# The last layer of a three-layer kernel as seven block products, with its operands loaded earlier and one item's transposes moved

## The chip, the core and the metric

The kernel runs on one core of one Trainium2 chip. TensorE does the matmuls and writes PSUM, which has eight banks here, b0 to b7, of 512 float32 columns on 128 partitions. VectorE (DVE) and ScalarE (ACT) work on SBUF and PSUM. SyncE (SP) issues every DMA. The metric is the device time of one execution in microseconds, given as the median of several runs. The trace is of one execution that was profiled.

## What is computed

```python
def _moe2_ref(x, w_in, w_out):
    h = x @ w_in
    g = h * (1.0 / (1.0 + np.exp(-h)))
    return (g @ w_out).astype(np.float32)
def reference(**kwargs):
    ...
    attn_out = _attn_ref(**attn_kwargs)
    ...
    x = np.ascontiguousarray(attn_out.transpose(0, 2, 1, 3)).reshape(B * S, H * D)
    x = _moe_ref(x=x, **moe_kwargs)
    return _moe2_ref(x=x, **moe2_kwargs)
```

Attention over 64 positions at a time comes first (4 sequences of 576 tokens, 8 heads of 64), then two pairs of layers: `_moe_ref` (512 to 2048 features, a leaky rectifier, back to 512) and `_moe2_ref`, shown above. There are 2304 tokens. The weights arrive as float64. "The last layer" below is `g @ w_out` of `_moe2_ref`, with 2304 x 2048 by 2048 x 512. "The third layer" is `x @ w_in` of the same function.

## The kernel before

Tokens are cut into 6 tiles of 384 (`TN`), the 2048 features into 16 blocks of 128. Every value of a matmul is split into two float32r parts, high and low: ScalarE casts the high part and VectorE subtracts it from the value (`parts`, L271 to L273). A product is then three matmuls: high by high, high by low, low by high.

Attention is 24 items, four for each tile. An item's scores (`mm_s`, L179), softmax (`softmax`, `rescale`), transposes (`mm_t`, L224, in two halves of three), the copies of these (`keep_t`) and the product with the values (`mm_v`, L240) are written out by hand: the first in the string `START`, the others inside the loop over the steps `f` of the first layer (`mlp_h1`, L334; `mlp_g1`; `join_g1`, L352). Item 8 (`EARLY`) is the first that stands in the loop: its transposes come at f = 0 of tile 1. Each engine works through its own instructions in the order in which the program issues them.

The third layer is already done by seven block products instead of eight: two tiles make a pair (`u`), `unit(u, c, ...)` computes four output blocks of 128 x 384 by `product` (L453, six matmuls of 128 x 384 each), and the eight units of a pair take their right sides from combinations of weights. Its results pass the Silu in `finish` (L468) and go to DRAM (L470). A hook between any two products runs what a table `plan` has for that slot: `slot(u, c, h)` counts seven slots for each unit. The weights of the last layer are converted beforehand (`aside`), kept in DRAM, and fetched and split during the third pair (`back`).

The last layer takes a tile at a time, with 16 blocks:

```python
        for n, (a, b) in enumerate(((gh, oh), (gh, ol), (gl, oh))):
            for i in banks:
                nc.tensor.matmul(acc2[t][i], a[:, i * P:(i + 1) * P], b,
```

`a` is the stationary operand, 128 columns of the Silu's output, and `b` the moving one, 128 x 512 of the weights. So a step is nine matmuls (L530), and `split_g2(n + 3)` runs three steps ahead. One product of the third layer, `last_product`, is done after the first step. At the end `put` copies the sums out (L539) and stores them.

Of the kernel before, what the change touches and what calls it, by code (L numbers as in the profile page):

```python
# [20 lines left out]
q0 w1 s0a q1 q2 s0b w2 s1a v0 s1b c1 q3 s2a v1 z s2b t0 h1 q4 s3a p0 v2 w3 s3b t1 c2 p1 v3 q5 s4a w4 s4b  # L21
t2 h2 v4 p2 s5a w5 s5b t3 v5 p3 c3 w6 s6a t4 s6b M0 p4 h3 G0 c4 s7a t5 s7b M1 p5 w7 G1 h4 t6
s8a M2 p6 s8b c5 G2 t7 M3 p7 h5 G3
# [8 lines left out]
def attention_two_mlps(ctx, tc, q, k, v, w_in1, w_out1, alpha, w_in2, w_out2, out):  # L32
# [186 lines left out]
    def mm_t(n):  # L219
        it = items[n]  # L220
        for hf in range(2):
# [4 lines left out]
    def keep_t(n):  # L226
        it = items[n]
        for hf in range(2):
# [243 lines left out]
    def last_product(prev):  # L472
        product(prev["u"], prev["c"], B22, prev["a"])
        finish(prev["u"], prev["c"], 0, 1, prev["a"], room(turn_c(), name="c"))
# [33 lines left out]
    gl2, gs2, acc2 = {}, {}, {}  # L508
    turn_2h, turn_2l = Turn(range(0, 4)), Turn(range(4, 8))

    def load_g2(n):
        if n >= NTILE * KF or n in gl2:
            return
        g = gl2[n] = stg.tile([P, TN], F32, name="gf", tag="st")
        nc.sync.dma_start(out=g, in_=gd2[divmod(n, KF)])

    def split_g2(n):
        if n >= NTILE * KF:
            return
        g = gl2.pop(n)  # L520
        gh, gl = room(turn_2h(), None, F32R, "gh"), room(turn_2l(), None, F32R, "gl")
        parts(g, gh, gl)
        gs2[n] = (gh, gl)

    def sums(t, f, banks):
        oh, ol = wt["o2", f]
        gh, gl = gs2[t * KF + f]
        for n, (a, b) in enumerate(((gh, oh), (gh, ol), (gl, oh))):
            for i in banks:
                nc.tensor.matmul(acc2[t][i], a[:, i * P:(i + 1) * P], b,  # L530
                                 start=(f == 0 and n == 0), stop=(f == KF - 1 and n == 2))

    def put(t, i, parts):
        r0 = t * TN + i * P
        w = DM // parts
        for j in range(parts):
            c = slice(j * w, (j + 1) * w)
            osb = cv.tile([P, w], F32, name="osb", tag="cv")
            (nc.scalar.copy if (i + j) % 2 else nc.vector.tensor_copy)(osb, acc2[t][i][:, c])  # L539
            nc.sync.dma_start(out=out[r0:r0 + P, c], in_=osb)  # L540

    def mlp_o2(t, f):
# [256 lines left out]
```

## Time and profile before

| | |
|---|---|
| median of 3 runs | 876.23 us (875.97 to 878.31) |
| the profiled execution | 877.78 us, of which the span of the trace is 876.0 us |
| TensorE busy | 846.5 us (97% of the span), 5472 matmuls and as many weight loads |
| VectorE, ScalarE busy | 489.0 us (56%), 414.0 us (47%) |

The span runs from the first to the last instruction of the trace. "PE" is TensorE's matmul, "PEld" its weight load, and "SPq" SyncE's queue of DMA issues. A busy time of an instruction reaches from its start to its end, so instructions that overlap count twice in a mean but not in a busy time.

### The profile page before, as it was taken

How to read it: one execution, taken by the hardware profiler on the slowest of the kernel's cores; microseconds unless marked ns; L12 is line 12 of the kernel's file. 1: busy time of each engine (PE TensorE's matmuls, PEld its weight loads, DVE VectorE, ACT ScalarE, POOL GpSimd, SP SyncE). 2: the span in 40 equal slices, each digit the busy share in tenths (PEclk: the TensorE clock that was granted, in tenths of full speed). 3: DMA queues.
4: the chain of work that ended last, by engine and by line, in shares of the span. 5: the costliest groups of instructions: out<-in, count | busy, mean ns of one | idle time of the engine just before them, and what ended most of it. 6: DMA issues, size and time to landing. Idle time of an engine off the chain costs nothing.

```text
span 876.0 us, 15271 instructions
## 1 busy us (share of the span) xinstructions
PE 846.5 (97%) x5472; PEld 794.2 (91%) x5472; DVE 489.0 (56%) x1193; ACT 414.0 (47%) x1080; POOL 3.1 (0%) x20
## 2 busy tenths in 40 slices
PE   5689999999999999999999999999999999999998
PEld 4569999999999999999999999999999888888886
DVE  5677875467676776567665474644644233233232
ACT  5576666667665532244323355645765322222221
POOL 1000000000000000000000000000000000000000
PEclk9899999999999999999999999999999999999999
DMA  8457743477655557765575345455565443344341
GB/s 263 155 154 248 217 141 127 131 244 218 216 176 190 160 182 251 266 193 192 195 255 158 111 156 180 157 204 192 192 193 179 124 134 120 112 131 124 110 129 61
DMA packets 103467, 152.01 MB, mean 174 GB/s; under 512 B 10336, under 2 KB 87392, under 8 KB 103392
## 3 DMA queue, kind: packets, MB, share of 16 engines
q1 hardware_dynamic: 103392, 151.04, 53.9%
q8 instruction: 43, 0.70, 0.3%
q14 instruction: 32, 0.26, 0.1%
HBM read 99.62 MB, written 51.38 MB: 172 GB/s over the span
## 4 chain that ended last, share of the span: by engine, by line
PE 91%; DVE 3%; ACT 3%; issue 2%; DMA 1%; SPq 0%; ACTq 0%; DVEq 0%
PE acc L395 23%; PE acc L530 22%; PE h L334 21%; PE qa L453 11%; PE qd L453 5%; PE pa L240 3%; PE qb L453 3%; PE pa L224 2%; PE pa L179 2%; ACT pr L198 1%; DMA kT<-in_k_dram 0%; DVE pr L193 0%; DVE cva L265 0%; ACT a L341 0%; ACT g L342 0%
## 5 line engine op out<-in xcount | busy, mean ns | idle before, releaser
L334 PE MATMUL h<-x,i 128*128 128x384 f32 x1152 | 207.4, 337 | 1.4 <-ACT g L342 1.4
L273 DVE TENSOR_TENSOR gl<-gf,gh 128x384 fp32r<-128x384 f32 x192 | 106.3, 556 | 171.2 <-PE acc L530 122.4
L334 PEld LDWEIGHTS h<-x,i 128*128 128x128 f32 x1152 | 199.0, 188 | 3.1 <-ACT g L342 2.7
L272 ACT CAST gh<-gf 128x384 fp32r<-128x384 f32 x192 | 97.7, 515 | 212.4 <-PE acc L530 124.8
L395 PE MATMUL acc<-gh,o 128*128 128x384 f32 x768 | 148.6, 334 | 0.0
L530 PE MATMUL acc<-o,gh 128*128 128x512 f32 x576 | 147.2, 389 | 0.0
L395 PEld LDWEIGHTS acc<-gh,o 128*128 128x128 f32 x768 | 134.5, 188 | 0.2 <-ACT gh L272 0.2
L530 PEld LDWEIGHTS acc<-o,gh 128*128 128x128 f32 x576 | 108.1, 188 | 22.3
L453 PE MATMUL qa<-v,w2i 128*128 128x384 f32 x576 | 108.2, 334 | 1.0 <-ACT fk L458 1.0
L453 PEld LDWEIGHTS qa<-v,w2i 128*128 128x128 f32 x576 | 100.5, 188 | 1.7 <-ACT fk L458 1.7
L395 PE MATMUL acc<-gl,o 128*128 128x384 f32 x384 | 82.0, 334 | 0.0
L530 PE MATMUL acc<-o,gl 128*128 128x512 f32 x288 | 81.8, 389 | 0.0
L341 ACT ACTIVATE a<-h 128x384 f32<-128x384 f32 x96 | 47.0, 490 | 69.1 <-PE h L334 49.3
L352 DVE SCALAR_TENSOR_TENSOR g<-a,nalpha,g 128x384 f32<-128x384 f32 x96 | 58.5, 614 | 33.2 <-ACT g L342 33.2
L395 PEld LDWEIGHTS acc<-gl,o 128*128 128x128 f32 x384 | 67.9, 188 | 0.0
L198 ACT ACTIVATE pr<-pr,nm 128x128 f32<-128x128 f32 x144 | 56.2, 395 | 24.5 <-DVE nm L193 24.5
L530 PEld LDWEIGHTS acc<-o,gl 128*128 128x128 f32 x288 | 54.1, 188 | 11.2
L453 PE MATMUL qd<-v,w2i 128*128 128x384 f32 x288 | 57.6, 334 | 0.0
L453 PEld LDWEIGHTS qd<-v,w2i 128*128 128x128 f32 x288 | 50.6, 188 | 0.0
L342 ACT ACTIVATE g<-h 128x384 f32<-128x384 f32 x96 | 46.6, 485 | 0.0
L265 DVE SCALAR_TENSOR_TENSOR cva<-s,cva 128x512 uint32<-128x512 uint32 x64 | 44.4, 693 | 2.2
L267 DVE SCALAR_TENSOR_TENSOR cva<-s,cva 128x512 uint32<-128x512 uint32 x64 | 44.3, 692 | 2.2
(64 smaller groups left out, 729.7 us busy)
## 6 DMA issues: line engine op xcount, KB each, us to landing
gf<-g SPq DMA_DIRECT2D x192, 192.0 KB, 2.4
g<-g SPq DMA_DIRECT2D x96, 192.0 KB, 3.9
g<-c SPq DMA_DIRECT2D x96, 192.0 KB, 1.9
s<-in_moe_w_in_dram SPq DMA_DIRECT2D x32, 512.0 KB, 5.2
s<-in_moe_w_out_dram SPq DMA_DIRECT2D x32, 512.0 KB, 4.8
ve<-in_v_dram SPq DMA_DIRECT2D x24, 192.0 KB, 3.7
x<-x SPq DMA_DIRECT2D x24, 192.0 KB, 2.0
xq<-x SPq DMA_DIRECT2D x12, 384.0 KB, 4.6
```

The source lines that it names most:

```text
L198: nc.scalar.activation(out=pr[:, j, :], in_=pr[:, j, :], func=AF.Exp, bias=nm[:, j:j + 1], scale=-1.0, accum_out=it["sm"][:, hf * HB + j:h ...
L265: nc.vector.scalar_tensor_tensor(out=a, in0=s[:, :, 1], scalar=0xC0000000, in1=a, op0=ALU.bitwise_and, op1=ALU.bitwise_or)
L267: nc.vector.scalar_tensor_tensor(out=a, in0=s[:, :, 0], scalar=29, in1=a, op0=ALU.logical_shift_right, op1=ALU.bitwise_or)
L272: nc.scalar.copy(hi, src)
L273: nc.vector.tensor_tensor(out=lo, in0=src, in1=hi.bitcast(F32), op=ALU.subtract)
L334: nc.tensor.matmul(h, w[:, kk, :], x, start=(kk == 0 and n == 0), stop=(kk == KD - 1 and n == 2))
L341: nc.scalar.activation(out=a, in_=h, func=AF.Relu, scale=-1.0)
L342: nc.scalar.activation(out=g, in_=h, func=AF.Relu)
L352: nc.vector.scalar_tensor_tensor(out=g, in0=a, scalar=nalpha[:, f:f + 1], in1=g, op0=ALU.mult, op1=ALU.add)
L395: nc.tensor.matmul(acc1[t][i], a[:, i * P:(i + 1) * P], b, start=(f == 0 and n == 0), stop=(f == KF - 1 and n == 2))
L453: nc.tensor.matmul(o, w[:, a, k0], b, start=start and kk == 0 and n == 0, stop=kk == 1 and n == 2, skip_group_check=True)
L530: nc.tensor.matmul(acc2[t][i], a[:, i * P:(i + 1) * P], b, start=(f == 0 and n == 0), stop=(f == KF - 1 and n == 2))
```

## The change

It has three parts.

The last layer is done by seven block products for each pair of tiles. The output of a pair is four blocks of 384 x 256. The left sides are blocks of the Silu's output (A11, A12, A22) and sums of them (S1 to S4), the right sides are blocks of the weights (B11, B21, B22) and combinations (T1 to T4) of 128 x 256. A product has 8 steps of nine matmuls of 128 x 256, so a pair has 56 steps and the layer 168. The order of the products is A11, S3, S2, A12, S1, A22, S4. Three of them start on empty banks, and four add to banks of an earlier one after a copy of it was taken (`fork2`). The right sides are combined in the earlier layers (`variants`) and kept in DRAM; 37 of the 56 are fetched and split in the third pair of the third layer and 19 (`late`) in the last layer.

The blocks A11 and A21 of the first pair are loaded in the third layer's last two units, from `slot(2, 6, 1)` on, and A22 and A12 in the last layer. `last_product` now comes after two steps.

The transposes are issued half by half. For items 0 to 7 the order of instructions stays the same on every engine. Item 8's move from f = 0 to f = 2.

```diff
-q0 w1 s0a q1 q2 s0b w2 s1a v0 s1b c1 q3 s2a v1 z s2b t0 h1 q4 s3a p0 v2 w3 s3b t1 c2 p1 v3 q5 s4a w4 s4b
+q0 w1 s0a q1 q2 s0b w2 s1a v0 s1b c1 q3 s2a v1 z s2b t0a t0b h1 q4 s3a p0 v2 w3 s3b t1a t1b c2 p1 v3 q5 s4a w4 s4b
...
+    STEPS = 7 * KH
+    SEQ = (A11, S3, S2, A12, S1, A22, S4)
+    gb, gs2, acc2, side2 = {}, {}, {}, {}
...
+    def load_g2(u, x, c):
...
+        gb[u, x, c] = g
+        nc.sync.dma_start(out=g, in_=gd2[2 * u + i, c + KH * jj])
...
+    def sum_g2(u, x, c):
...
+        a, b, op, o = {S3: (A11, A21, ALU.subtract, None), S1: (A21, A22, ALU.add, A21),
+                       S2: (S1, A11, ALU.subtract, A11), S4: (A12, S2, ALU.subtract, S2)}[x]
...
+        nc.vector.tensor_tensor(out=o, in0=gb[u, a, c], in1=gb[u, b, c], op=op)
+        gb[u, x, c] = o
...
+        if n < 4:
+            t = tp.tile([P, 2, TN], F32R, name="gs", tag="ts") if n == 0 else stg.tile([P, 2, TN], F32R, name="gs", tag="st")
+            gh, gl = t[:, 0, :], t[:, 1, :]
+        else:
+            r = turn_gs()
+            gh, gl = room(r, None, F32R, "gh"), room(r + 1, None, F32R, "gl")
+        parts(gb[u, x, c], gh, gl)
         gs2[n] = (gh, gl)
...
+    def sums(n, chunks):
...
+        gh, gl = gs2[n]
+        w = wt["o2", c, v]
+        for a, b in ((gh, 0), (gh, 1), (gl, 0)):
+            for i in chunks:
+                nc.tensor.matmul(acc2[u, v][i], a[:, i * P:(i + 1) * P], w[:, b, :],
...
+    def banks2(u, v):
+        at = {A11: (2, 3) if u % 2 else (4, 6), A12: (7, 1), S3: (5, 0)}[v]
+        x, y = bank(at[0], "acc"), bank(at[1], "acc")
+        side2[u, v] = (x, y[:, :HD])
+        acc2[u, v] = (x[:, :HD], x[:, HD:], y[:, :HD])
...
+    def fork2(u, v):
...
+        for o, c in zip(side2[u, v], (slice(0, 2 * HD), slice(2 * HD, 3 * HD))):
+            nc.scalar.copy(s[:, c], o)
+        return s
...
+    def put(u, i, j, v, s=None, part=(0, 1)):
...
+            if s is not None:
+                nc.vector.tensor_tensor(out=x, in0=o, in1=x, op=ALU.add)
+            elif k == 0:
+                nc.scalar.copy(x, o)
+            else:
+                nc.vector.tensor_copy(x, o)
...
+        if n >= NU * STEPS - 3:
+            if n < NU * STEPS - 1:
...
             for i in range(NC):
+                for nn in range(n - 2, n + 1):
+                    sums(nn, (i,))
+                if i:
+                    put(u, 0, 1, v, None, (i - 1,))
...
+        if v == A11:
+            forks["p1"] = fork2(u, v)
...
+        elif v == A12:
+            put(u, 0, 0, v, forks["p1"])
+        elif v == S3:
+            forks["p7"] = fork2(u, v)
+        elif v == S2:
+            forks["u2"] = fork2(u, v)
+        elif v == S1:
+            put(u, 1, 1, v, forks["p7"])
+        elif v == A22:
+            put(u, 1, 0, v, forks["u2"])
+        else:
+            put(u, 0, 1, v)
...
+    def around2(n):
+        u, m = divmod(n, STEPS)
+        for x, first in ((A11, 36), (A21, 32), (A22, 40), (A12, 48)):
+            if 0 <= m - first < KH:
+                load_g2(u + 1, x, m - first)
+        if u == 0 and 4 <= n < 4 + KH:
+            load_g2(0, A12, n - 4)
+        for x, first in ((S3, -4), (S1, 2), (S2, 7), (S4, 34)):
+            for uu in (u, u + 1):
+                c = n - (uu * STEPS + first)
+                if uu == 0 and x == S3:
+                    continue
+                if uu == 0 and x in (S1, S2):
+                    c -= 2 if x == S1 else 3
+                if 0 <= c < KH:
+                    sum_g2(uu, x, c)
...
         elif x == "t":
-            mm_t(n)
-            keep_t(n)
+            hf = (int(w[-1] == "b"),)
+            rescale(n, hf)
+            mm_t(n, hf)
+            keep_t(n, hf)
...
+        def combine():
...
+            combos(x[:, :HD], x[:, HD:], y[:, :HD], y[:, HD:], t)
+            d = dram.tile([P, 7, HD], F32, name=f"w2o_{c}")
+            nc.sync.dma_start(out=d[:, 0, :], in_=x[:, :HD])
+            nc.sync.dma_start(out=d[:, 1:3, :], in_=y.rearrange("p (k d) -> p k d", d=HD))
+            nc.sync.dma_start(out=d[:, 3:, :], in_=t)
...
         def fetch():
+            a = held["o2", m] = cv.tile([P, HD], F32, name="cva", tag="cv")
+            nc.sync.dma_start(out=a, in_=parked[c, v])
...
+        def split():
+            s = wroom((56 + m) % 64, [P, 2, HD], F32R, "w2o")
+            parts(held.pop(("o2", m)), s[:, 0, :], s[:, 1, :])
+            wt["o2", c, v] = s
+        return fetch, split
...
+    late = list(range(4 * KH, 4 * KH + 3)) + list(range(5 * KH, 7 * KH))
+    for i, m in enumerate(m for m in range(7 * KH) if m not in late):
+        plan.setdefault(slot(2, 0, 3) + i * 9 // 8, []).append(rights[m][0])
+        plan.setdefault(slot(2, 1, 0) + i * 9 // 8, []).append(rights[m][1])
...
-                    rescale(n, (1,) if n == EARLY else (0, 1))
-                    mm_t(n)
+                    if n > EARLY:
+                        rescale(n)
+                        mm_t(n)
                     if f:
                         keep_v(n - 1)
-                    keep_t(n)
+                    if n > EARLY:
+                        keep_t(n)
...
+                    if n == EARLY:
+                        for hf in ((0,), (1,)):
+                            rescale(n, hf)
+                            mm_t(n, hf)
+                            keep_t(n, hf)
                     rescale(n + 1)
...
-        plan.setdefault(slot(2, 6, 3 + i), []).append(lambda i=i: load_g2(i))
+    at = lambda g, f: plan.setdefault(g, []).append(f)
+    for i, c in enumerate(range(KH)):
+        at(slot(2, 6, 1) + i * 3 // 4, lambda c=c: load_g2(0, A11, c))
+        at(slot(2, 6, 6) + i * 3 // 4, lambda i=i: load_g2(0, A21, i))
     for i in range(3):
-        plan.setdefault(slot(2, 7, 3 + i), []).append(lambda i=i: (split_g2(i), load_g2(i + 4)))
+        if i < 2:
+            at(slot(2, 7, 4) + i, lambda i=i: split_g2(i))
+        at(slot(2, 7, 2) + i, lambda i=i: sum_g2(0, S3, i))
 
...
-    for n in range(NTILE * KF):
+    finish(prev["u"], prev["c"], 1, 1, c22)
+    split_g2(2)
+    for n in range(NU * STEPS):
+        if n == 2:
+            last_product(prev, stg.tile([P, TN], F32, name="c", tag="st"))
+            for c in range(KH):
+                load_g2(0, A22, c)
         split_g2(n + 3)
-        load_g2(n + 7)
-        mlp_o2(*divmod(n, KF))
-        if n == 0:
-            last_product(prev)
-            finish(prev["u"], prev["c"], 1, 1, c22)
+        around2(n)
+        if n < 5:
+            sum_g2(0, S3, 3 + n)
+        for i, m in enumerate(late):
+            if n == 14 + i * 30 // len(late):
+                rights[m][1]()
...
+        step2(n)
+        for i, m in enumerate(late):
+            if n == 12 + i * 30 // len(late):
+                rights[m][0]()
```

On TensorE the order at the ninth item (number 8; `pa<-ident,pr` are its transposes, `h<-x,i` the first layer's matmuls) was, before:

```order
L240 MATMUL pa<-pt,ve 64x64 x2
L179 MATMUL pa<-kT,qT 64x128 x12
L224 MATMUL pa<-ident,pr 128x128 x6
L334 MATMUL h<-x,i_277 128x384 x2
L334 MATMUL h<-x,i_278 128x384
L334 MATMUL h<-x,i_277 128x384 x2
```

and the same transposes now stand here:

```order
L335 MATMUL h<-x,i_450 128x384
L335 MATMUL h<-x,i_449 128x384 x2
L335 MATMUL h<-x,i_450 128x384
L224 MATMUL pa<-ident,pr 128x128 x6
L335 MATMUL h<-x,i_647 128x384 x2
L335 MATMUL h<-x,i_648 128x384
```

The transposes have moved behind the h products of two steps, 24 matmuls, of which the last ones are shown, and stand ahead of the third.

On TensorE the end of the third layer (`qa<-v,w2i`) and the start of the last (`acc<-o` before, `acc<-w2o` now; `gs` holds both parts of one of the first four left sides) was:

```order
L453 MATMUL qa<-v,w2i 128x384 x12
L530 MATMUL acc<-o_7730,gh 128x512 x3
L530 MATMUL acc<-o_7731,gh 128x512 x3
L530 MATMUL acc<-o_7730,gl 128x512 x3
L453 MATMUL qa<-v,w2i 128x384 x6
L530 MATMUL acc<-o_7766,gh 128x512 x3
```

and is now:

```order
L454 MATMUL qa<-v,w2i 128x384 x12
L564 MATMUL acc<-w2o,gs 128x256 x18
L454 MATMUL qa<-v,w2i 128x384 x6
L564 MATMUL acc<-w2o,gs 128x256 x18
L564 MATMUL acc<-w2o,gh 128x256 x6
L564 MATMUL acc<-w2o,gl 128x256 x3
```

One step of nine matmuls of 512 columns ahead of the last third-layer product has become two steps of nine matmuls of 256.

On VectorE the first tiles of the last layer (`gl` is the low part of a left side, `osb` a result that is copied out) were:

```order
L463 TENSOR_TENSOR c<-qa,fk 128x384
L273 TENSOR_TENSOR gl<-gf,gh 128x384 x16
L539 COPY osb<-acc 128x512 x2
L273 TENSOR_TENSOR gl<-gf,gh 128x384 x16
L539 COPY osb<-acc 128x512 x2
```

and at the start of the second pair VectorE now has (the rows with `g<-g` and `s<-g` are the sums S1, S2 and S3):

```order
L539 TENSOR_TENSOR s_9611<-g 128x384
L539 TENSOR_TENSOR g<-g 128x384
L274 TENSOR_TENSOR gl<-g,gh 128x384
L539 TENSOR_TENSOR s_9627<-g 128x384
L539 TENSOR_TENSOR g<-g 128x384
L274 TENSOR_TENSOR gl<-g,gh 128x384
L539 TENSOR_TENSOR g<-g 128x384
L274 TENSOR_TENSOR gl<-s_9507,gh 128x384
L539 TENSOR_TENSOR g<-g 128x384
L274 TENSOR_TENSOR gl<-s_9524,gh 128x384
L539 TENSOR_TENSOR g<-g 128x384
L274 TENSOR_TENSOR gl<-s_9541,gh 128x384
```

Up to two sums have come between one split and the next.

## Rows read from the trace of the kernel before

**Rows 1.** The page: the head, and the chain that ended last by line.
```profile
span 876.0 us, 15271 instructions
...
PE acc L395 23%; PE acc L530 22%; PE h L334 21%; PE qa L453 11%; PE qd L453 5%; PE pa L240 3%; PE qb L453 3%; PE pa L224 2%; PE pa L179 2%; ACT pr L198 1%; DMA kT<-in_k_dram 0%; DVE pr L193 0%; DVE cva L265 0%; ACT a L341 0%; ACT g L342 0%
```

**Rows 2.** Busy time by stage; start and end, length, engines with instructions, granted clock.
```profile
300.00:486.00 186.00, 186.00 (x1074) 185.77 (x1073) 123.09 (x249) 66.84 (x153) 0.00 (x0) 1.00 0.66 213
486.00:680.00 194.00, 192.98 (x1107) 191.65 (x1106) 99.45 (x192) 107.82 (x243) 0.00 (x0) 1.00 0.52 175
675.19:872.34 197.15, 197.15 (x871) 163.04 (x870) 59.81 (x106) 52.19 (x103) 0.00 (x0) 1.00 0.39 119
```

**Rows 3.** Timeline, TensorE, last layer: start, length, what, how many.
```profile
675.19 1.55 PE L530 MATMUL acc<-o,gh 128*128 128x512 f32 x6
680.42 1.52 PE L530 MATMUL acc<-o,gh 128*128 128x512 f32 x6
682.46 1.52 PE L530 MATMUL acc<-o,gh 128*128 128x512 f32 x6
```

**Rows 4.** Timeline, TensorE, third layer.
```profile
663.75 1.20 PE L453 MATMUL qa<-v,w2i 128*128 128x384 f32 x6
664.79 1.20 PE L453 MATMUL qd<-v,w2i 128*128 128x384 f32 x6
```

**Rows 5.** Slices of 10 ns: weight loads under way (x) in the first layer.
```profile
106.14:106.15 0.01, 0.01 (x1) 1.00 0.99 410
106.24:106.25 0.01, 0.01 (x2) 1.00 1.40 563
106.41:106.42 0.01, 0.01 (x1) 1.00 0.93 308
106.42:106.43 0.01, 0.01 (x2) 1.00 1.27 461
```

**Rows 6.** VectorE and ScalarE by form: busy time, mean ns of one.
```profile
L273 DVE TENSOR_TENSOR gl<-gf,gh 128x384 fp32r<-128x384 f32 x192 | 106.3, 556 | 171.2 <-PE acc L530 122.4 <-ACT gh L272 40.9 <-PE acc L395 7.6
L463 DVE TENSOR_TENSOR c<-qd,fk 128x384 f32<-128x384 f32 x24 | 13.3, 554 | 11.7 <-PE qd L453 8.5 <-ACT c L468 3.2
L273 DVE TENSOR_TENSOR w2i<-ts,w2i 128x256 fp32r<-128x256 f32 x32 | 13.4, 419 | 7.5 <-ACT w2i L272 7.5
L539 DVE COPY osb<-acc 128x512 f32<-128x512 f32 x11 | 7.1, 687 | 9.7 <-PE acc L530 9.7
L341 ACT ACTIVATE a<-h 128x384 f32<-128x384 f32 x96 | 47.0, 490 | 69.1 <-PE h L334 49.3 <-issue 16.0 <-ACT gh L272 1.7
```

**Rows 7.** Timeline, VectorE: two operations back to back.
```profile
674.08 0.55 DVE L463 TENSOR_TENSOR c<-qd,fk 128x384 f32<-128x384 f32 x1
674.55 0.55 DVE L273 TENSOR_TENSOR gl<-gf,gh 128x384 fp32r<-128x384 f32 x1
```

**Rows 8.** Timeline, TensorE and VectorE, around the ninth item's transposes.
```profile
63.76 0.55 PE L224 MATMUL pa<-ident,pr 128*128 128x128 f32 x3
66.34 0.52 PE L224 MATMUL pa<-ident,pr 128*128 128x128 f32 x3 [2.03 <-DVE pr L216]
...
64.69 0.61 DVE L352 SCALAR_TENSOR_TENSOR g<-a,nalpha,g 128x384 f32<-128x384 f32 x1
65.63 0.56 DVE L216 TENSOR_TENSOR pr<-pr,rs 128x384 f32<-128x384 f32 x1
```

**Rows 9.** Timeline, the end of the program.
```profile
871.95 0.39 PE L530 MATMUL acc<-o,gl 128*128 128x512 f32 x1
872.38 0.43 DVE L539 COPY osb<-acc 128x256 f32<-128x256 f32 x1 [2.03 <-PE acc L530]
872.84 0.37 ACT L539 COPY osb<-acc 128x256 f32<-128x256 f32 x1 [1.91 <-DVE osb L539]
```

**Rows 10.** The page: DMA issues; size, median us from issue to landing.
```profile
gf<-g SPq DMA_DIRECT2D x192, 192.0 KB, 2.4
s<-in_moe_w_out_dram SPq DMA_DIRECT2D x32, 512.0 KB, 4.8
```

More of the change, by code (lines that the diff above doesn't have):

```diff
@@ L217, in rescale, with mm_t @@
                                     op=ALU.mult)
-    def mm_t(n):
+    def mm_t(n, halves=(0, 1)):
         it = items[n]
-        for hf in range(2):
+        for hf in halves:
             pb = it[f"b{hf}"] = att_bank()
@@ L224, in mm_t, with keep_t @@
                 nc.tensor.transpose(pb[:, j * P:(j + 1) * P], it[f"p{hf}"][:, j, :], ident)
-    def keep_t(n):
+    def keep_t(n, halves=(0, 1)):
         it = items[n]
-        for hf in range(2):
+        for hf in halves:
             pt = it[f"pt{hf}"] = room(turn_pt(), [P, HB, P], F32, "pt")
@@ L517, in split_g2 @@
     def split_g2(n):
-        if n >= NTILE * KF:
+        if n >= NU * STEPS:
             return
-        g = gl2.pop(n)
-        gh, gl = room(turn_2h(), None, F32R, "gh"), room(turn_2l(), None, F32R, "gl")
-        parts(g, gh, gl)
-        gs2[n] = (gh, gl)
[L525 to L542, printed above, removed]
-        if f == 0:
-            acc2[t] = [bank(i, "acc") for i in ((1, 5, 0) if t % 2 else (4, 6, 7))]
-        if t == NTILE - 1 and f >= KF - 3:
-            if f == KF - 1:
-                for i, ff in ((0, 2), (0, 1), (1, 2), (1, 1), (0, 0), (1, 0), (2, 2), (2, 1), (2, 0)):
-                    sums(t, f - ff, [i])
-                    if ff == 0:
-                        put(t, i, 2 if i == NC - 1 else 1)
-            return
-        sums(t, f, range(NC))
-        if f == KF - 1:
-            for i in range(NC):
-                put(t, i, 1)
+        u, m = divmod(n, STEPS)
@@ new lines, in attention_two_mlps, with step2 @@
+    ready = []
+    forks = {}
+    def step2(n):
+        u, m = divmod(n, STEPS)
+        k, c = divmod(m, KH)
+        v = SEQ[k]
+        if c == 0:
+            if v in (A11, A12, S3):
+                banks2(u, v)
+            elif v == A22:
+                acc2[u, v], side2[u, v] = acc2[u, S3], side2[u, S3]
+            else:
+                acc2[u, v], side2[u, v] = acc2[u, A11], side2[u, A11]
+        if n >= NU * STEPS - 3:
+            if n < NU * STEPS - 1:
+                return
+            for i in range(NC):
+                for nn in range(n - 2, n + 1):
+                    sums(nn, (i,))
+                if i:
+                    put(u, 0, 1, v, None, (i - 1,))
+            return
+        sums(n, range(NC))
+        if c < KH - 1:
+            return
+        if v == A11:
[8 more added lines that the diff above has]
+            put(u, 1, 1, v, forks["p7"])
+        elif v == A22:
+            put(u, 1, 0, v, forks["u2"])
+        else:
+            put(u, 0, 1, v)
@@ new lines, in around2 @@
+    def around2(n):
+        u, m = divmod(n, STEPS)
+        for x, first in ((A11, 36), (A21, 32), (A22, 40), (A12, 48)):
[12 more added lines that the diff above has]
+                    sum_g2(uu, x, c)
@@ L558, in attention_two_mlps @@
     in1 = [plain_steps("i1", w_in1, f, 0) for f in range(KF)]
     out1 = [plain_steps("o1", w_out1, f, 32) for f in range(KF)]
-    out2 = [plain_steps("o2", w_out2, f, 56) for f in range(KF)]
     done = {}
@@ L657, in attention_two_mlps @@
     weights2(3, 56, 64)
-    aside(range(8, 12), 64, 74)
+    variants(3, 64, 69)
+    variants(4, 69, 74)
     weights2(4, 74, 85)
@@ L662, in attention_two_mlps @@
     weights2(7, slot(0, 2, 3), slot(0, 5, 0))
-    aside(range(12, 16), slot(1, 1, 0), slot(1, 4, 0))
     for u in range(NU - 1):
```

86 lines of the change are left out of this document (59 added, 27 removed).

## The prediction

> **What bounds the kernel now.** I read the page first. The chain that ended last is TensorE nearly throughout, and the last layer's line L530 holds 22% of the span [rows 1]. Then I asked for the busy time by stage. In the last layer TensorE is busy for all of its 197.15 us at a granted clock of 1.00, while VectorE is busy for 59.8 and ScalarE for 52.2; in the third layer TensorE misses 1 us of 194 [rows 2]. So what the last layer costs is the number of its matmuls times the time from one to the next, and the timeline gives that second number. A step of nine matmuls of 512 columns starts at 680.42, the next at 682.46: 226.7 ns each [rows 3]. In the third layer six of 384 columns take from 663.75 to 664.79: 173.3 ns each [rows 4]. The 128 columns between the two sizes cost 53.3 ns, which is the 2.4 GHz level, and what is left at either size is 13.3 ns. The last layer before is then 864 x 0.2267 = 195.8, plus 1.04 for the one third-layer product inside it, and 0.3 of seams: 197.15.
>
> **The change, part by part.**
>
> *The matmuls of the last layer.* 864 matmuls of 512 columns become 3 pairs x 7 products x 8 steps x 9 = 1512 of 256 columns: 12.5% fewer columns, but 75% more matmuls, so the 13.3 ns is paid more often. No row has 256 columns with a 128-column float32r load, so the price is bounded. From the line through the two sizes it is 106.7 + 13.3 = 120.0 ns. The lower end is 106.7, if the fixed part vanished; the upper end is the 173.3 of 384 columns. What decides between them is the weight load, since each matmul loads its own 128 columns and has only 107 ns to hide the next load in. Where TensorE starts again after a stop in the first layer, the first load is under way at 106.14 and the second joins it at 106.24; the third waits until 106.42, when the queue has settled to the matmuls' own pace [rows 5]. So loads can follow each other within 0.10 us or a little more, which is just inside 120 ns. I take 120.0: 1512 x 0.1200 = 181.4, which is **14.4 us less** (bounds: 34.5 less to 66.2 more).
>
> The Trainium skill has a rule for this, in "TensorE: Matmul & The Clock Gate", section "Back-to-back issue gap": columns over 2.4 plus 2.5 ns when warm. By it a 512-column matmul would take 215.8 ns where the row shows 226.7, so I go by the row; by the rule the new layer would be 1512 x 109.2 = 165.1, 30.7 us less than the layer before.
>
> *What feeds these matmuls.* VectorE's work in the last layer grows from one subtraction for each 2.04 us to this: 166 splits at 556 ns, 93 sums at 554 ns (96 less the three done earlier), 19 weight splits at 419 ns, 9 additions of 512 columns at 687 and 9 of 256 near 419, 3 copies near 430 [rows 6, 9]. That is 163 us of 182, nearly the bound. But these durations overlap: two 384-column operations back to back start 0.47 us apart, at 674.08 and 674.55 [rows 7], so it is rather 138 us. The densest place is the first 16 steps of the second and third pair: 16 splits, 4 sums S3, 8 S1, 8 S2, 36 operations. At 0.47 and with one copy they need 17.3 us, exactly the 16 x 1.08 us that TensorE takes; at 0.555 they need 20.4, and VectorE is 3.1 us behind. The cushion is the lead of three steps: the buffers of step n + 3 come free when step n - 1 ends, its low part is wanted three steps and six matmuls later, 3.96 us, and a cast (0.49, the size of L341) and a subtraction (0.556) take 1.05 of it [rows 6], so 2.9 us may be lost. I take no stall; the upper end is 2 x 3.1 = 6 us for the two pairs. A bank is copied after its product and written again eight or more steps, 8.6 us, later, against about 1.1 us for the copies: nothing.
>
> *The seam.* SyncE issues A22's eight loads only after the store of the last third-layer product, which ends at 675.19 + 2.16 + 1.04 = 678.4; with the Silu (0.49) the store goes at about 679, and the first block lands 2.4 us after its issue [rows 10], near 682. VectorE stands at its first S1 from step 4 (680.6) on; behind it waits the split of step 8, whose low part is wanted at 685.6. From 682 on there are a sum, a sum and a split: ready at 683.5. If the landing took 4.8 us, as the slowest kind here does [rows 10], it would be 685.8, and TensorE would wait 0.2. The 16 early loads, six stores and some fetches share about 10 us of the third layer's end on SyncE, which is tight, but S3 wants its last block only at step 4. I charge **0.4 us** for the seam (0 to 3).
>
> *The earlier layers.* Combining the weights adds 8 x 4 subtractions of 256 columns (419 ns), 13.4 us on VectorE, five eighths of it in the second layer and the rest in the third, and 37 weight splits of 256 columns replace 16 of 512. VectorE is busy 123 of 186 us and 99 of 194 us there, and TensorE for all but 1 us [rows 2]: that idle time covers it, and I charge nothing. If that cover were gone, a late subtraction would hold a blend or a split, up to the 1.7 us of one block's four.
>
> *The moved transposes.* Today TensorE does the first half of item 8's transposes at 63.76 and then waits 2.03 us for VectorE's rescaling of the second half, until 66.34 [rows 8]. In the new order it goes on with 24 h matmuls, 4.2 us, to 67.9. The rescaling now stands behind VectorE's softmax of item 9 and one more join. That join needs the first h product (65.8) and its two ReLUs of 0.49 [rows 6], so starts at 66.8 or later; from a join's start to the end of the rescaling were 64.69 to 66.19, 1.5 us [rows 8]. So it ends at 68.3 or somewhat later, and TensorE wants it at about 68.3. I leave a wait of 0.6, so **1.4 us less** (0 to 2.03). The next item's transposes come two steps later, so nothing is queued up behind these. For items 0 to 7 the order is as before: nothing.
>
> *The end.* Now the last matmul ends at 872.34, two copies of 256 columns follow one another, until 873.21, and the span ends 2.79 later [rows 9]. With one copy of 256 columns behind the last matmul: **0.4 us less** (0 to 0.4).
>
> The sum: -14.4 + 0.4 - 1.4 - 0.4 = -15.8. The profiled execution had 877.78, 1.78 of it outside the span, so its like would be 862.0; the median of the runs stands 1.55 below that execution, so 860.4.
>
> **The rivals.**
>
> *Late feeding.* VectorE falls behind in the dense steps, or the seam's loads come late: 3 to 12 us given back, 863.5 to 872. For it: durations that add up to 163 of 182 us, and an in-order queue in which one sum that waits for a load holds all splits behind it. Against it: the spacing of 0.47 and 2.9 us of lead.
>
> *The load becomes the bound, and the kernel gets slower.* The place is TensorE in the last layer. If a 128-column load can't be hidden under 256 columns, the time from one matmul to the next rises above 120, and each ns costs 1.51 us. From 130.5 ns on nothing is gained ((195.8 + 1.4) / 1512). Midway to the third layer's 173.3, at 146.7, the layer takes 221.8 and the kernel about 901. For it: no row has the load so poorly covered. Against it: the second load 0.10 us after the first [rows 5]. By the skill's page, section "LDWEIGHTS (loading the stationary operand)", a load takes its columns over 1.2, 106.7 ns here; with rows 5 the trace agrees, and it would leave the load just hidden.
>
> *The fixed part shrinks.* If 256 columns paid less than 13.3 ns, the layer could come down to 161.3 and the kernel to about 840. The 2.5 ns of the Trainium skill's page would give 844. Two rows of different size with the same 13.3 speak against it.
>
> *The matmuls gain as forecast, but nothing shows.* Something of 12 us or more in the earlier layers would be needed; their idle TensorE time leaves no sign of it.
>
> **How the numbers follow.** The forecast (857 to 863.5) gets 0.72; late feeding 0.15; the load as the bound 0.07, most of it slower; the smaller fixed part 0.04; no visible gain 0.02. The predicted time is 860.4. The range 856 to 868 takes in the forecast and over half of late feeding. A measurement of this kernel can tell 0.3%, 2.6 us, from no change. Faster by more: 0.72 + 0.15 + 0.04 = 0.91; slower by more: 0.06; the rest, 0.03, is neither.
>
> **What would show it.** In the new profile a step of nine matmuls of 256 columns should take 1.08 us (a step of 1.18 makes the prediction wrong, and tells the load as the cause if the weight loads stand end to end). The last layer should be about 183 us from its first matmul to its last. TensorE's waits for VectorE in the last layer should be under 1 us in all; if not, late feeding holds. The wait of L224 for the rescaling should fall from 2.03 to below 1. The third layer should keep its 173.3 ns and its 1 us of idle time.

## The result, and the profile after

The changed kernel took 862.82 us by the median (861.72 to 863.76, 4 runs), the kernel before 877.1 (875.97 to 878.31, 4 runs): a ratio of 0.9837, 95% interval 0.9816 to 0.9857. Run again later (below), it took 861.47 against 877.05, 0.9827 (0.9813 to 0.9841). Both lie in the predicted range, above the predicted 860.4.

The page of the changed kernel: the span, the busy times of the engines, and the chain that ended last by line. L564 is the last layer's matmul now, L454 the third layer's.

```profile
span 859.9 us, 17181 instructions
...
PE 829.6 (96%) x6120; PEld 811.4 (94%) x6120; DVE 589.1 (69%) x1442; ACT 461.0 (54%) x1206; POOL 3.1 (0%) x20
...
PE acc L396 22%; PE h L335 21%; PE acc L564 20%; PE qa L454 11%; PE qd L454 5%; PE pa L241 3%; PE qb L454 3%; PE pa L224 2%; PE pa L179 2%; ACT pr L198 1%; DMA x<-x 1%; DMA kT<-in_k_dram 1%; DMA g<-g 1%; DMA cva<-w2o 0%; DVE pr L193 0%
```

The bound is where it was, and VectorE has gone from 489.0 to 589.1 us of work. Busy time of the changed kernel over the whole last layer, and over 16 steps from shortly ahead of the second pair on; columns as in [rows 2], in the order PE, PEld, DVE, ACT, POOL.

```profile
672.54:856.67 184.13, 183.27 (x1519) 182.57 (x1518) 147.49 (x305) 98.54 (x210) 0.00 (x0) 1.00 0.42 135
733.10:750.40 17.30, 17.30 (x146) 17.30 (x146) 16.75 (x37) 9.25 (x19) 0.00 (x0) 1.00 0.28 100
```

The layer went from 197.15 [rows 2] to 184.13. In the dense stretch VectorE is busy for 16.75 of 17.30 us, and TensorE doesn't stop. The timeline of TensorE where the last layer has found its pace:

```profile
679.08 0.88 PE L564 MATMUL acc<-w2o,gh 128*128 128x256 f32 x6
679.80 0.52 PE L564 MATMUL acc<-w2o,gl 128*128 128x256 f32 x3
680.16 0.88 PE L564 MATMUL acc<-w2o,gh 128*128 128x256 f32 x6
680.88 0.52 PE L564 MATMUL acc<-w2o,gl 128*128 128x256 f32 x3
681.24 0.88 PE L564 MATMUL acc<-w2o,gh 128*128 128x256 f32 x6
```

Nine matmuls take from 679.08 to 680.16: 120.0 ns each, the number that was read off the line through 226.7 and 173.3 [rows 3, 4]. By the formula of the Trainium skill ("TensorE: Matmul & The Clock Gate", section "Back-to-back issue gap"), columns over 2.4 plus 2.5 ns, the estimate would be 109.2; the trace doesn't agree. The section gives that formula for an isolated matmul, and says that in a stream with a weight load for each matmul both set the pace. The prediction left this condition out.

At the seam to the third layer it waits once. TensorE, then VectorE (the sums S3 are `s<-g`), then SyncE's issues of the loads that these sums read:

```profile
668.38 1.20 PE L454 MATMUL qa<-v,w2i 128*128 128x384 f32 x6
669.42 1.20 PE L454 MATMUL qd<-v,w2i 128*128 128x384 f32 x6
670.46 2.24 PE L454 MATMUL qa<-v,w2i 128*128 128x384 f32 x12
672.54 0.87 PE L564 MATMUL acc<-w2o,gs 128*128 128x256 f32 x6
674.21 1.82 PE L564 MATMUL acc<-w2o,gs 128*128 128x256 f32 x12 [0.80 <-DVE gs L274]
675.87 1.23 PE L454 MATMUL qa<-v,w2i 128*128 128x384 f32 x6
...
672.07 1.16 DVE L539 TENSOR_TENSOR s<-g 128x384 f32<-128x384 f32 x2 [2.87 <-DMA g<-g]
673.14 0.55 DVE L464 TENSOR_TENSOR c<-qd,fk 128x384 f32<-128x384 f32 x1
673.61 0.55 DVE L274 TENSOR_TENSOR gs<-g,gs 128x384 fp32r<-128x384 f32 x1
...
681.89 1.03 DVE L539 TENSOR_TENSOR s<-g 128x384 f32<-128x384 f32 x2 [0.36 <-DMA g<-g]
...
666.67 2.74 SPq L526 DMA_DIRECT2D g<-g  x5
```

The third layer's six still take 1.04 us (668.38 to 669.42), as in [rows 4]. The low part that TensorE wants at 673.4 (`gs`, 673.61) stands on VectorE behind a sum that waits 2.87 us for a block of A21. That block's load, the second of the five at 666.67, is issued at 667.3 and lands 4.8 us later, twice the 2.4 us of [rows 10]. The seam costs more than the idle 0.80: the 18 matmuls ahead of the third layer's last product take 3.33 us (672.54 to 675.87) where 18 x 0.1200 would be 2.16, so 1.17 are lost. The wait for A22 that the prediction charged comes at 681.89, lasts 0.36, and holds nobody up.

Around item 8's transposes (L224), with item 9's scores ahead and item 10's behind (L179), the kernel before and then the changed one:

```profile
62.94 0.89 PE L179 MATMUL pa<-kT,qT 64*64 64x128 f32 x24
...
75.98 0.89 PE L179 MATMUL pa<-kT,qT 64*64 64x128 f32 x24
```

```profile
61.36 0.89 PE L179 MATMUL pa<-kT,qT 64*64 64x128 f32 x24
...
67.67 0.52 PE L224 MATMUL pa<-ident,pr 128*128 128x128 f32 x3 [0.72 <-DVE sm L212]
...
73.15 0.89 PE L179 MATMUL pa<-kT,qT 64*64 64x128 f32 x24
```

The wait of 2.03 [rows 8] is 0.72 now, and from one scores to the next pass 11.79 us, no longer 13.04. (The bracket names L212, a neighbour on VectorE; the rescaling that these transposes need, L216, runs there from 66.96 to 67.52.) But item 9's scores already start 1.58 earlier, ahead of anything that the change moves on any engine. That is the start of this one execution and not the change. Nearly all of it arises in one stretch, in which the granted clock (the third number from the end) differs; the kernel before, then the changed one:

```profile
51.20:54.50 3.30, 3.30 (x45) 2.85 (x44) 2.10 (x4) 3.18 (x11) 0.00 (x0) 0.50 0.88 292
```

```profile
51.20:54.50 3.30, 3.30 (x55) 2.89 (x50) 2.34 (x7) 3.18 (x11) 0.00 (x0) 1.00 0.89 289
```

The 0.50 is 1.2 GHz, the 1.00 is 2.4 GHz. Just before, up to 50.5, TensorE had stood idle for 1.90 us in the one execution and 1.75 in the other. The same matmuls start 0.10 us apart in the two traces ahead of this stretch (51.26 and 51.16), the six transposes in it take 1.54 and 0.87 us, and behind it the starts are 1.58 apart (55.98 and 54.40).

The whole account of the two profiled executions: start -1.58, transposes -1.25, from item 10's scores to the last layer +0.18 (599.21 and 599.39), last layer -13.02, what follows its last matmul -0.43 (3.66 and 3.23), outside the span +0.04: -16.06, from 877.78 to 861.72. Without the start it is -14.5, which is near what the medians show (-14.3).

### The profile page after: what moved, and what is told of

Same layout as the page of the kernel before. It is cut to its first block, busy times and chain, and to the rows that moved or that the text cites. A ratio compares the mean times of both kernels' runs of the same rounds, so it can differ in the third digit from the quotient of the medians.

```text
span 859.9 us, 17181 instructions
## 1 busy us (share of the span) xinstructions
PE 829.6 (96%) x6120; PEld 811.4 (94%) x6120; DVE 589.1 (69%) x1442; ACT 461.0 (54%) x1206; POOL 3.1 (0%) x20
## 4 chain that ended last, share of the span: by engine, by line
PE 88%; DVE 4%; ACT 3%; DMA 3%; issue 2%; SPq 0%; ACTq 0%; DVEq 0%
PE acc L396 22%; PE h L335 21%; PE acc L564 20%; PE qa L454 11%; PE qd L454 5%; PE pa L241 3%; PE qb L454 3%; PE pa L224 2%; PE pa L179 2%; ACT pr L198 1%; DMA x<-x 1%; DMA kT<-in_k_dram 1%; DMA g<-g 1%; DMA cva<-w2o 0%; DVE pr L193 0%
## 5 line engine op out<-in xcount | busy, mean ns | idle before, releaser
L564 PE MATMUL acc<-w2o,gh 128*128 128x256 f32 x984 | 145.5, 283 | 0.1
L564 PEld LDWEIGHTS acc<-w2o,gh 128*128 128x128 f32 x984 | 130.3, 192 | 0.3 <-ACT gh L273 0.3
L454 PE MATMUL qa<-v,w2i 128*128 128x384 f32 x576 | 108.2, 335 | 0.9 <-ACT fk L459 0.8
L454 PEld LDWEIGHTS qa<-v,w2i 128*128 128x128 f32 x576 | 100.4, 188 | 1.5 <-ACT fk L459 1.5
L273 ACT CAST gh<-gf 128x384 fp32r<-128x384 f32 x96 | 48.2, 514 | 85.6 <-PE acc L396 39.5
L564 PE MATMUL acc<-w2o,gl 128*128 128x256 f32 x492 | 86.7, 283 | 0.0
L273 ACT CAST gh<-g 128x384 fp32r<-128x384 f32 x116 | 58.5, 513 | 47.8 <-PE acc L564 44.4
L274 DVE TENSOR_TENSOR gl<-g,gh 128x384 fp32r<-128x384 f32 x116 | 63.5, 556 | 26.7 <-ACT gh L273 25.3
L274 DVE TENSOR_TENSOR gl<-gf,gh 128x384 fp32r<-128x384 f32 x96 | 52.5, 555 | 35.0 <-ACT gh L273 32.4
L564 PEld LDWEIGHTS acc<-w2o,gl 128*128 128x128 f32 x492 | 71.3, 192 | 0.0
L454 PE MATMUL qd<-v,w2i 128*128 128x384 f32 x288 | 57.7, 334 | 0.0
L454 PEld LDWEIGHTS qd<-v,w2i 128*128 128x128 f32 x288 | 50.6, 188 | 0.0
```

Of the source, the lines that this page charges most:

```text
L273: nc.scalar.copy(hi, src)
L274: nc.vector.tensor_tensor(out=lo, in0=src, in1=hi.bitcast(F32), op=ALU.subtract)
L454: nc.tensor.matmul(o, w[:, a, k0], b, start=start and kk == 0 and n == 0, stop=kk == 1 and n == 2, skip_group_check=True)
L564: nc.tensor.matmul(acc2[u, v][i], a[:, i * P:(i + 1) * P], w[:, b, :], start=v in (A11, A12, S3) and c == 0 and a is gh and b == 0 and i != 1,
```

## The experiments

Each trace was cut at the same four places, so that a difference can be put where it belongs. All in us; "scores 9" is the start of item 9's scores.

| kernel | scores 9 | to scores 10 | to the last layer | last layer |
|---|---|---|---|---|
| before | 62.94 | 13.04 | 599.21 | 197.15 |
| changed | 61.36 | 11.79 | 599.39 | 184.13 |
| transposes alone | 62.80 | 11.79 | 599.79 | |
| last layer alone | 61.61 | 13.02 | 601.68 | 183.58 |
| sums behind splits | 62.56 | 11.80 | 599.47 | 183.32 |
| both waits | 60.35 | 10.88 | 599.21 | 183.04 |
| narrow | 62.62 | 11.80 | 599.30 | 173.18 |
| VectorE load | 62.80 | 11.77 | 600.45 | 189.54 |
| VectorE load doubled | 59.92 | 11.79 | 599.24 | 210.18 |
| no rest | 63.24 | 11.80 | 600.10 | 184.96 |
| changed, again | 60.92 | 11.80 | 600.28 | 183.42 |
| both waits, again | 60.68 | 10.90 | 601.40 | 183.53 |
| loads behind stores | 60.38 | 11.80 | 599.19 | 184.23 |
| all waits | 61.47 | 10.87 | 599.19 | 183.55 |

**The two parts apart.** First the kernel before with only item 8's transposes moved:

```diff
-                    rescale(n, (1,) if n == EARLY else (0, 1))
-                    mm_t(n)
+                    if n > EARLY:
+                        rescale(n)
+                        mm_t(n)
...
+                    if n == EARLY:
+                        for hf in ((0,), (1,)):
+                            rescale(n, hf)
+                            mm_t(n, hf)
+                            keep_t(n, hf)
```

> The kernel before with one part of the change: item 8's transposes at f = 2 instead of f = 0. My theory, that the reordering replaces a wait of 2.03 us by one of 0.72 and that nothing later takes this back: TensorE's wait for the rescaling falls to 0.7, and the time by 1.3 us, ratio 0.9985. Rival, that the 2.65 us by which the last layer starts earlier in the changed kernel's trace all come from this move: 2.6 us, ratio 0.997. Rival, that a later stage takes it back: ratio 1.000.

876.06 us (11 runs) against 877.78 (15 runs), ratio 0.9978 (0.997 to 0.9987). The interval takes in the 0.9985 of the theory and, at its edge, the 0.997 of the first rival, so only the trace decides between them. Then the changed kernel with these lines taken back:

> The changed kernel with item 8's transposes back at f = 0. My theory, that 1512 x 120.0 instead of 864 x 226.7 ns is nearly all of the gain: about 13 us less than before, ratio 0.985, and TensorE's wait of about 2 us for the rescaling is back. Rival, that the earlier start of the last layer is more than the transposes' 1.3 us: 2.6 us slower than the changed kernel, ratio 0.9865 or more.

863.91 us, ratio 0.9842 (0.9828 to 0.9855). Its wait is the old one again, and ends on the rescaling:

```profile
65.00 0.52 PE L224 MATMUL pa<-ident,pr 128*128 128x128 f32 x3 [2.03 <-DVE pr L216]
```

The transposes are worth 1.25 and 1.23 us by the table, in the two directions, and the last layer the rest. The 601.68 us that this trace takes to the last layer, 2.29 more than the changed kernel's, come up below.

**The seam.** The first pair's eight sums S3 are put behind the splits of the last layer's first steps:

```diff
-        at(slot(2, 7, 2) + i, lambda i=i: sum_g2(0, S3, i))
...
-        if n < 5:
-            sum_g2(0, S3, 3 + n)
+        if n < KH:
+            sum_g2(0, S3, n)
```

> The changed kernel with the first pair's eight sums S3 one in each of the last layer's steps 0 to 7, so that none of them stands in VectorE's queue ahead of the first splits. My theory, that the wait of 0.8 us at the seam (low part of the first left side) comes from VectorE standing at the first S3 for A21's load: the wait is gone, the third layer's last matmul and the last layer's second six follow without a gap, 0.8 to 1.0 us less than the changed kernel. Rival of the prediction, that the seam is set by A22's loads behind the last store: the wait stays.

862.21 us, ratio 0.9816 (0.9798 to 0.9833). TensorE's first 18 matmuls now stand together:

```profile
671.75 2.24 PE L454 MATMUL qa<-v,w2i 128*128 128x384 f32 x12
673.83 2.31 PE L564 MATMUL acc<-w2o,gs 128*128 128x256 f32 x18
675.98 1.21 PE L454 MATMUL qa<-v,w2i 128*128 128x384 f32 x6
```

TensorE has no idle time left in the last layer, and the layer is 0.81 shorter: the sums did hold the split. (The two medians, 862.21 and 862.82, are too close to show it.) At the seam itself 1.18 are gained, 2.15 us for the 18 matmuls instead of 3.33. Part of it comes back between 687 and 699, where the moved sums crowd VectorE: the six matmuls from 691.14 to 692.09 take 0.95 instead of 0.72, because the low part that follows is ready only at 692.04. Such delays don't show as idle time, since a matmul's record is 0.28 long and the next one starts after 0.12. Next, the same with the rescaling of item 8's second half ahead of item 9's softmax:

```diff
+                    if n == EARLY:
+                        rescale(n, (1,))
                     softmax(n + 1, 1)
```

> The same with item 8's second rescaling moved ahead of item 9's second softmax half on VectorE, so that it is done before the transposes' turn. My theory: the wait of 0.72 us falls below 0.1, and with the seam mended the kernel takes about 1.6 us less than the changed one, ratio to before 0.982. Rival, that the softmax half which now waits delays item 9's transposes: the wait turns up there, and only the seam's 0.9 us are gained.

861.25 us, ratio 0.9807 (0.979 to 0.9825). The six transposes are one piece, and scores 9 to scores 10 take 10.88:

```profile
65.44 0.82 PE L224 MATMUL pa<-ident,pr 128*128 128x128 f32 x6
```

**The price of a matmul.** Columns of the moving operand are left out: 224, 192 and 128 of 256 are done in the three pairs, except where a bank starts.

```diff
+        cols = slice(0, HD if c == 0 and v in (A11, A12, S3) else (224, 192, 128)[u])
...
-                nc.tensor.matmul(acc2[u, v][i], a[:, i * P:(i + 1) * P], w[:, b, :],
+                nc.tensor.matmul(acc2[u, v][i][:, cols], a[:, i * P:(i + 1) * P], w[:, b, cols],
```

> The changed kernel with fewer columns in the last layer's moving operand: 224 in the first pair, 192 in the second, 128 in the third (the first step of a product that starts a bank keeps 256); the columns left out are not computed. Theory that the moving columns set the pace and a load hides under 256 of them with room to spare: 106.7, 93.3 and 66.7 ns from one matmul to the next. Theory that the load of 128 columns was just hidden: the pace stops falling near 107 to 120 ns whatever the width, so that the second and third pair take as long as each other, and 224 columns are hardly faster than 256.

851.96 us in one run. The timeline of TensorE in the three pairs:

```profile
680.77 0.83 PE L565 MATMUL acc<-w2o,gh 128*128 128x224 f32 x6
681.44 0.50 PE L565 MATMUL acc<-w2o,gl 128*128 128x224 f32 x3
681.78 0.83 PE L565 MATMUL acc<-w2o,gh 128*128 128x224 f32 x6
...
745.03 0.83 PE L565 MATMUL acc<-w2o,gh 128*128 128x192 f32 x6
...
746.03 0.83 PE L565 MATMUL acc<-w2o,gh 128*128 128x192 f32 x6
...
802.46 0.83 PE L565 MATMUL acc<-w2o,gh 128*128 128x128 f32 x6
...
803.47 0.83 PE L565 MATMUL acc<-w2o,gh 128*128 128x128 f32 x6
```

Nine take 1.00 to 1.01 us in all three, 111.7 ns each, whether 224 columns move or 128. By the prediction's line it would be 106.7, 93.3 and 66.7. So there is a floor at 111.7 that doesn't depend on the moving columns. What stays the same in the three is the 128-column load. In the second pair loads (the number behind TensorE's) are under way without a gap, and VectorE, busy for 45.68 of 55.00 us, isn't the limit:

```profile
735.00:790.00 55.00, 55.00 (x494) 55.00 (x494) 45.68 (x93) 30.08 (x61) 0.00 (x0) 1.00 0.45 144
```

Loads without a gap prove little, since they have none at 256 columns either (17.30 of 17.30 above): their records are 0.19 us long and overlap. A fixed price of this size for any load with its matmul is out, as the 24 scores of item 9, each with a load of 64 columns, pass in 0.89 us. So that the floor is the load's is argued, not shown. By the Trainium skill ("TensorE: Matmul & The Clock Gate", section "LDWEIGHTS (loading the stationary operand)") a load would need 106.7 ns by estimate, 5 less than the floor.

**VectorE's cover.** An addition of 320 columns that nobody reads is put on VectorE in every second step of the last layer:

```diff
+        if n % 2:
+            nc.vector.tensor_tensor(out=extra, in0=extra, in1=extra, op=ALU.add)
```

> The changed kernel with one more VectorE operation (320 columns, about 0.40 us, its result not used) in every second step of the last layer, 84 in all. Theory that VectorE's work is the 147 us of 184 which the trace shows as busy, and that the lead of three steps covers the dense places: 34 us more fit into the idle time, TensorE's waits stay under 3 us in all, at steps 0 to 15 of the second and third pair alone. Theory that VectorE is already the bound by the sum of its durations, 163 us: all of it is added, 20 us or more.

869.62 us in one run, the layer 5.41 longer. That is more than the first theory's 3 and far less than the second's 20, and of TensorE's six new waits four stand in the first pair (695 to 728), where none was expected. Then in every step:

> The same operation in every step, 168 in all, 67 us. By the busy time VectorE then has 214 us for a layer of 183: it becomes the bound, the layer takes 210 to 218 us and the kernel is slower than before the change. By the sum of durations it would be 163 + 82 = 245 us.

886.19 us in one run, the layer 26.05 longer. Busy times by stretches of the last layer, first with the addition in every second step, then in every step:

```profile
740.00:760.00 20.00, 19.52 (x161) 19.23 (x161) 20.00 (x45) 10.11 (x21) 0.00 (x0) 1.00 0.19 66
760.00:780.00 20.00, 20.00 (x168) 19.93 (x168) 16.77 (x38) 10.72 (x23) 0.00 (x0) 1.00 0.13 35
```

```profile
820.00:840.00 20.00, 17.59 (x121) 14.94 (x120) 20.00 (x45) 8.13 (x18) 0.00 (x0) 1.00 0.00 0
```

and VectorE's timeline in that last stretch:

```profile
822.12 0.56 DVE L539 TENSOR_TENSOR g<-g 128x384 f32<-128x384 f32 x1
822.58 0.56 DVE L274 TENSOR_TENSOR gl<-g,gh 128x384 fp32r<-128x384 f32 x1
823.05 0.50 DVE L896 TENSOR_TENSOR extra<-extra 128x320 f32<-128x320 f32 x1
823.45 0.56 DVE L539 TENSOR_TENSOR g<-g 128x384 f32<-128x384 f32 x1
```

Back to back, a 384-column operation costs 0.47 and the extra one 0.40. The doubled load is 168 x 0.40 = 67.2 of work, and the layer grew by 26.05, so about 41 us of room were used up: the layer's own work on VectorE is at most about 210.2 - 67.2 = 143 us, an estimate, beside the 138 of the prediction and the 163 of added durations. But the room can't be used evenly. With 33.6 us added the sum is at most 177 of 184, and still 5.41 were lost, in stretches where VectorE has no gap (740 to 760), while it stood idle 3.2 us in the next. The cover is thin in the dense stretches, and the change does not exceed it.

**The order of the products.** In the second pair alone S4 follows S1 at once, on the same banks, and A22 comes last:

```diff
-    SEQ = (A11, S3, S2, A12, S1, A22, S4)
+    ORDERS = (SEQ, (A11, S3, S2, A12, S1, S4, A22), SEQ)
...
-        for x, first in ((A11, 36), (A21, 32), (A22, 40), (A12, 48)):
+        for x, first in ((A11, 36), (A21, 32), (A22, 48 if u == 1 else 40), (A12, 48)):
```

The third pair's loads of A22 come eight steps later with it.

> The changed kernel with S4 directly behind S1 in the second pair alone (A22 last), so that the banks to which S1 added are written again with no product between. Theory that the order's rest is what keeps TensorE from waiting: it waits there once, for the two additions that read these banks, 1.0 to 1.6 us, and the kernel is that much slower. Rival, that the copies hide under the matmuls' own lead or the loads: no wait.

865.17 us in one run. The last layer is 0.83 longer than the changed kernel's, with one new wait:

```profile
782.08 0.98 PE L565 MATMUL acc<-w2o,gh 128*128 128x256 f32 x6 [0.96 <-DVE fk L590]
```

TensorE waits 0.96, a little less than expected, for VectorE's addition that reads the bank. The copies took "about 1.1" in the prediction; eight steps between two uses of a bank hide that whole. The rest of the 3.5 us by which its span is longer than that of the changed kernel lies in its start (1.88) and ahead of the last layer (0.71).

**What hides the last two gains.** The changed kernel and the version without both waits were run once more on one chip.

> The changed kernel once more, as the yardstick for the next run on the same chip. 862.3 to 863.3 us by the median, a ratio of 0.983 to 0.984. Nothing is tested by it alone; its first scores of the tenth item should start anywhere between 60 and 63 us if the spread of the start is chance.

> The changed kernel with its two remaining waits taken out. If these waits (0.8 us at the seam, 0.7 us ahead of the transposes, with what trails them) are on the path, it is 1.5 to 2.1 us faster than the changed kernel of the same call, 860.5 to 861.2. Rival: part of it was the luck of the earlier runs, and it is within 0.5 us of the changed kernel.

861.47 us (860.74 to 862.42) and 861.77 (859.69 to 864.96): no difference, though the two waits are gone from the trace (10.90 between the scores, 18 matmuls in one piece at the seam). The table shows where it went. The last layer is no shorter, 183.53 and 183.42: the seam cost this execution of the changed kernel only 0.8, and the late low parts cost the other 0.9. (In the mean of four traces each, moving the sums takes the layer from 183.84 to 183.36.) And it is 601.40 to the last layer, 1.12 more than in the changed kernel beside it. In the second layer TensorE waits for a cast, and ScalarE had stood ahead of it for the store of the fourth tile's result (`x<-x`, whose landing frees a buffer). TensorE and ScalarE in the second run, then ScalarE before the change:

```profile
440.77 1.69 PE L396 MATMUL acc<-gh,o 128*128 128x384 f32 x8 [1.44 <-ACT gh L273]
...
439.83 0.48 ACT L403 COPY x<-acc 128x384 f32<-128x384 f32 x1 [8.34 <-DMA x<-x]
```

```profile
440.87 0.48 ACT L402 COPY x<-acc 128x384 f32<-128x384 f32 x1 [5.23 <-DMA x<-x]
```

SyncE's queue suggests why. Here are the two loads for a combination of last-layer weights and the four stores, in the changed kernel, and below it in the kernel before:

```profile
431.63 1.19 SPq L259 DMA_DIRECT2D s<-in_moe_w_out_dram  x2
...
433.99 6.43 SPq L404 DMA_DIRECT2D x<-x  x4
```

```profile
434.38 0.74 SPq L258 DMA_DIRECT2D s<-in_moe_w_out_dram  x1
...
436.73 5.04 SPq L403 DMA_DIRECT2D x<-x  x4
```

The change needs weight blocks in twos, 512 KB each, and their loads go just ahead of these stores. In the ten traces so far with this order ScalarE waits 6.37 to 8.34 there; before the change, and with the transposes alone, 5.23 and 5.36. In six of the ten, not in that of the changed kernel's first execution, TensorE then waits at about 440, from 0.15 to 1.44. Moved by one slot, the loads are behind the stores:

```diff
-    variants(4, 69, 74)
+    variants(4, 70, 74)
```

> The changed kernel with the fifth pair of weight loads for the last layer issued after the stores of the second layer's fourth tile, one slot later, and no longer ahead of them. If these two loads of 512 KB are what makes the stores slow, ScalarE's wait for them near 440 us falls from 6.65 to 8.34 to 5.5 or less, as before the change, TensorE has no wait for the cast behind it, and from the eleventh item's scores to the last layer pass 599.2 to 599.6 us. By the median it is up to 0.8 us faster than the changed kernel, 861 to 862. Rival: the stores are slow for another reason (the blocks that are loaded behind them); then the wait stays at 6.6 or more and TensorE's wait of 0.1 to 1.4 comes back in about half of the runs.

861.85 us (860.63 to 863.41), ratio 0.9833 (0.9816 to 0.9849).

```profile
437.06 0.48 ACT L403 COPY x<-acc 128x384 f32<-128x384 f32 x1 [5.23 <-DMA x<-x]
```

ScalarE's wait is 5.23 again, TensorE has none there, and 599.19 pass to the last layer, where the ten traces had 599.21 to 601.68, 600.05 in the mean. The median, 861.85, doesn't show it. The profiled execution, 860.63, waited 1.21 at the seam, the longest wait of all at that place. Last, all of these together, with the next weight loads behind the next tile's stores as well (`weights2(5, 86, 96)` for `weights2(5, 85, 96)`):

> The version with both waits taken out (the early rescaling, the sums behind the splits), and the loads behind the stores as in the run beside it, for the next tile's stores too. If all three waits are on the path, 860.0 to 861.2 us by the median, and no wait of TensorE between the eleventh item and the end of the last layer but those for the third layer's first blends (1.0 to 1.4 in all). Rival: something else turns up in the second layer, and it is not faster than 861.5.

860.14 us (859.4 to 860.24), ratio 0.9808 (0.9794 to 0.9822), the lowest median of these runs. The interval overlaps those of the changed kernel, so a gain over it is likely but not shown. ScalarE's waits for the two tiles' stores are 5.46 and 4.11; the second was 6.13 to 8.10 in all other traces, 6.74 in the kernel before. From the second layer to the end TensorE stands idle only for the third layer's first blends, 1.2 us.

## Why the prediction was nearly right

*The matmuls of the last layer: right.* 120.0 ns a matmul, 14.4 us. The lower bound of 106.7 could have been set higher from the trace before: the transposes, which load 128 columns and move 128, start 109 ns apart there (76.96 to 77.40 us, granted clock 1.00), and so do the first two loads of [rows 5] (106.140 and 106.249). The rival of the load as the bound is nearer than its chance of 0.07 says: the floor of 111.7 is 8.3 ns below. The smaller fixed part is out, and so are 109.2 ns.

*What feeds them: right.* In the changed kernel TensorE has no wait for VectorE outside the seam, and the spacing of 0.47 was the price to take. Late feeding did not happen, but 0.2 us a step more makes it happen.

*The seam: right in kind, wrong block and too small.* The step that failed is "S3 wants its last block only at step 4". True for TensorE, but two sums stand on VectorE ahead of the split whose low part step 0 wants, and they wait for A21, whose first block took 4.8 us to land. The layer should have taken 183.2 by the prediction's terms (181.4 + 1.04 + 0.3 + 0.4) and took 184.13. Of the difference the seam is about 0.8 (1.17 lost where 0.4 was charged); another 0.3 is lost at 724, where a cast of ScalarE's stands behind that of a weight block whose load it waits for, 1.95 us. In seven traces of this order the idle wait at the seam is 0.33 to 0.85, and 1.21 in an eighth. Putting the sums later removes it and makes some low parts late instead.

*The earlier layers: the zero doesn't hold in every execution.* VectorE's added subtractions are hidden, as the prediction said: TensorE waits for VectorE nowhere in these two layers. What it left out is SyncE: loads of the new weight blocks ahead of stores that free a buffer. It cost TensorE nothing in the profiled execution, and up to 1.4 at that place in others. A second place, the fifth tile's stores near 470, cost 1.26 in one trace and 0.13 to 0.18 in four, of which one has the transposes alone; there the loads are the old ones. Behind the stores, in the last version, they leave ScalarE its shortest wait there, 4.11; why it reaches 8.10 in one of the others stays open.

*The moved transposes: right.* 1.25 where 1.4 was predicted, a wait of 0.72 for 0.6, behind item 9's softmax, as worked out.

*The end: right.* 0.43 for 0.4.

*From the profiled execution to the median: wrong by 2.65.* The prediction took 1.55 off because the median of three runs stood that far below; the profiled execution of the changed kernel stood 1.1 below its median instead. Other medians of the kernel before are 877.1, 877.78, 877.05 and 876.31. The start alone spreads over 3.3 us (59.92 to 63.24).

*The sum: 1.3 too large.* -15.8 was forecast, and without the start it was -14.5; most of the difference is the last layer's. That the 862.0 for the profiled execution meets the measured 861.72 is luck, since the start gave 1.58.

## What to carry to other kernels

When a product is cut finer to save columns, read the time from matmul to matmul at two sizes, draw the line to the new size, and look for the floor: here 12.5% fewer columns made the layer 6.6% shorter, and the next cut would meet 111.7 ns. Follow every moved load along the whole queue of its engine: what costs is the in-order neighbour (a sum ahead of a split, a load ahead of a store), not the step that wants the data. When single gains are smaller than the spread of a run, cut each trace at fixed places and compare stretches.

## What the runs showed of the hardware

The floor of 111.7 ns for float32r matmuls with a 128-column load each, the same at 224, 192 and 128 moving columns; above it columns over 2.4 plus 13.3 ns, at 256, 384 and 512 columns (120.0, 173.3 and 226.7).

The start of item 9's scores differs by 3.3 us between executions of code that is the same up to there. The granted clock between 20 and 40 us doesn't tell it: it was 0.80 in the second run of the changed kernel and 0.59 in that of the version without both waits, with starts of 60.92 and 60.68. The clock between 50 and 60 us tells two groups apart: it is 0.83 in the six traces that start at 62.56 to 63.24, and 1.00 in the eight that start at 59.92 to 61.61. The idle time of TensorE just before was 1.90 to 1.92 us in the six and 1.75 to 1.77 in the eight. Both groups hold versions of the changed kernel. Whether the idle time decides the clock isn't shown, and what sets the 1.7 us of spread within the eight stays open.
